# Two expert layers behind an attention: the first layer's weight loads are placed earlier, its first copies get another buffer, and the output words' low parts change engine

## The chip, the cores and the metric

One Trainium2 chip, one core of it. The metric is the device time of one execution in microseconds (us), the median of several runs. A core has five engines that run their own instruction lists in order and wait for each other by semaphores: TensorE (PE; its weight loads are PEld), VectorE (DVE), ScalarE (ACT), GpSimd (POOL) and SyncE (SP), which here issues nearly all DMA transfers. A row "SPq" is SP's sequencer issuing a transfer; the transfer itself goes on after it.

## The reference

```python
def _attn_ref(q, k, v, M_prev, z_prev, beta):        # 4 x 8 heads x 576 x 64
    scores = causal(q @ k.T / sqrt(D)); a = softmax(scores); local = a @ v
    q_p = elu(q) + 1
    mem_out = (q_p @ M_prev) / (q_p @ z_prev + 1e-6)
    return sigmoid(beta) * mem_out + (1 - sigmoid(beta)) * local

def _moe_ref(x, w_gate, w_val, w_out):               # x: 2304 x 512
    return sigmoid(x @ w_gate) * (x @ w_val) @ w_out # 512 x 1536, 512 x 1536, 1536 x 512

def _moe2_ref(x, w_gate, w_val, w_out):
    g = x @ w_gate
    return g * sigmoid(g) * (x @ w_val) @ w_out
```

The weights arrive as 64-bit floats and the kernel turns them into 32-bit ones itself. It computes each matrix product as three passes over a high and a low part of each factor (high by high, high by low, low by high).

## The kernel before

Attention comes first, with the first layer's value product for part of the tokens and the turning of its gate and value weights woven in; turned weights are **kept** in DRAM (`ws`), and value results as words in DRAM (`vs`). Then come four stages on which this text rests:

**Blocks of layer 1** (`blocks`, from L844). 24 runs: for each of six weight pairs p (256 columns of the gate or value weights) three gate runs and one value run over 768 tokens each. A run is seven products (Strassen's scheme; `product`, L828), each of six matmuls of 128 x 128 by 128 x 384. A run has three of eight PSUM banks. What frees a bank is a copy on ACT into a tile c0, c1 or c2 (`keep`, L874), an addition on DVE (`add`, L877), or the finish: the sigmoid on ACT (L837) and a multiplication on DVE (L839 by value words loaded as `vi`, L841 by the other run's result). Finished results are stored (`hs`, L845).

What else has to be done meanwhile stands in a table `at`: a step under the number n is emitted after product n of the list. Products of one weight pair p are numbered b = 28p and on. Per pair there are four such jobs:

- V: load of the kept value weights (`kept`, L595, two transfers `raw<-ws`), two sums steps (L633, L634, L637, L638, on DVE), and eight splits: high parts on ACT (L31, `wset`), low parts on DVE (L654);
- G: the same for the next pair's gate weights;
- W0 and W1: two output words (128 rows of `w_out`) loaded raw (L487), turned by one ACT step (L500) and DVE steps (L503 and L504, L507, L511), and stored (`ws<-a`, L562).

All four jobs load into two buffers `raw` by turns, so a load on SP waits until the job before the last has read its buffer for the last time; everything behind it in SP's list waits too. Inside this stage the emission order is binding on every engine (`pinned`).

**Output of layer 1** (`outputs`, L974): for each of six token tiles twelve words m; the words are loaded two at a time (L582; the last two raw, L487) and put as a high part (ACT, L31) and a low part (L603, on POOL) into places of a matmul operand that has come free (`xop`, `wset`). **Blocks and output of layer 2** are built alike (PE lines L828 and L971) with loads from DRAM in another pattern.

Tiles lie in pools that are opened and closed like a stack. A pool that is opened over the place of a closed one waits, tile by tile, for the last use of that place. At the start of the blocks of layer 1 the pool `m_h` (five tiles h of 3 KB per partition) is opened first, and `m_c` (c0, two c1, c2, 1.5 KB each) behind it.

Of the kernel before, what the change touches and what calls it, by code (L numbers as in the profile page):

```python
ENGINE = {'wh': 'act', 'xh': 'pool', 'vo': 'act', 'ml': 'pool', 'p0': 'act', 'p3': 'act', 'e': 'dve', 'p2': 'any', 'x': 'act', 'mh': 'pool', 'p4': 'dve', 'w': 'pool', ('head', 'w'): 'pool', 'xl': 'pool', ('rest', 'e'): 'act', ('rest', 'p4'): 'act', 'p1': 'act', 'th': 'act', 'uh': 'act', ('rest', 'x'): 'any', ('head', 'n3'): 'pool', 'n3': 'pool', ('rest', 'n4'): 'pool', ('rest', 'n3'): 'pool', ('head', 'n1'): 'pool', 'n4': 'dve', ('head', 'p3'): 'dve', ('rest', 'p3'): 'act', ('head', 'n0'): 'dve', 'oh': 'act', 'ol0': 'dve', 'ol1': 'dve', 'xg': 'act', 'xm': 'dve', 'w00': 'dve', 'w01': 'dve', 'w10': 'dve', 'w11': 'dve', 'hv': 'dve'}
WHEN = {'qk': -2.918, 'zm': -2.8, 'v': -0.622, 'pe': -1.766, 'pw': -1.489, 'pm': -1.092, 't0': -0.87, 't1': -0.45, 'te': 0.857, 's3': 0.004, 's2': 0.265, 's4': 0.5, 's1': 0.704, 's0': 0.85, 'p3': 0.476, 'p2': 0.809, 'p4': 0.938, 'p1': 0.919, 'p0': 1.1, 'v0': 1.112, 'v1': 1.339, 'store': 1.26, ('rest', 'v0'): 1.425, ('rest', 's4'): 0.378, ('head', 'v'): -1.263, ('rest', 'p1'): 0.628, ('rest', 's1'): -0.002, ('head', 'v0'): 1.122, ('rest', 'store'): 2.346, ('head', 's2'): 0.45, ('rest', 's0'): 0.08, ('head', 's4'): 0.733, ('rest', 'v1'): 1.114, ('rest', 'zm'): -2.421, ('rest', 'te'): 0.827, ('rest', 'pw'): -1.506}
WHEN0 = {'pm': -1.252, 'pe': -1.0, 'pw': -0.99, 'zm': -2.0, 't0': -1.2, 's0': 0.834, 'te': 0.682}
SPAN = {'head': (0.8, 0.85), 'rest': (0.734, 0.75), 'full': (0.866, 1.0)}
# [2 lines left out]
REUSE = dict(reuse_waits="tile")  # L7
# [11 lines left out]
F32 = mybir.dt.float32  # L19
# [20 lines left out]
def either(nc, name):  # L40
    return nc.gpsimd if ENGINE.get(name, "pool") == "pool" else nc.vector

# [431 lines left out]
class Weights:  # L474
# [123 lines left out]
    def put(self, l, m, s, t, a):  # L598
        def high():
            copy(self.nc, "wh", t[:, 0], a)  # L600

        def low():
            either(self.nc, "wl").tensor_sub(t[:, 1], a, t[:, 0].bitcast(F32))  # L603
            self.ready[l, m, s] = t.rearrange("p a (k f) -> p a k f", f=128)

        return [high, low]
# [67 lines left out]
class Moe:  # L674
# [344 lines left out]
    def run(self, att, banks):  # L1019
        nc, MC, NP, NJ, T = self.nc, self.MC, self.NP, self.NJ, self.T  # L1020
# [55 lines left out]
            return do  # L1076

        with ExitStack() as tiles:
            self.hp = self.pool("m_h", 5, tiles, **REUSE)
            self.cs = _Bufs(self.pool("m_c", 1, tiles, **REUSE), dict(c0=1, c1=2, c2=1))  # L1080
            top = ExitStack()
            self.scr = self.pool("m_scr1", 4, top, **REUSE)

            runs = []
            for p in range(NP):
                order = [(0, 0), (0, 2), (1, 2), (0, 1)] if p == 0 else [(0, 0), (0, 1), (0, 2), (1, 2)]
                runs += [Run(0, s, p, j, sets, s == 0 and j < 2) for s, j in order]
            at = {}

            steps = self.right(self.from_dram(1), 1, xo[2])  # L1090
            for half, a, b in ((steps[:8], 6, 12), (steps[8:], 15, 21)):
                put(at, half[:1], a - 6 if a < 15 else a - 2, a)
                put(at, half[1:], a, b)
            for p in range(NP):

                b = 28 * p
                if p:
                    turning, splits = prepare(0, p, 1)
                    put(at, turning[:1], b + 3, b)
                    put(at, turning[1:], b + 7, b + 9)  # L1100
                    put(at, splits, b + 10, b + 18)
                    load, turn = W.keep_output(0, 2 * p - 2, False)
                    put(at, load, b + 4, b)
                    put(at, turn, b + 9, b + 15)
                if p + 1 < NP:
                    turning, splits = prepare(0, p + 1, 0)
                    put(at, turning[:1], b + 18, b)
                    put(at, turning[1:], b + 22, b + 24)
                    put(at, splits, b + 25, b + 30)
                if p:  # L1110
                    load, turn = W.keep_output(0, 2 * p - 1, False)
                    put(at, load, b + 19, b)
                    put(at, turn, b + (23 if p + 1 < NP else 21), b + (30 if p + 1 < NP else 25))

            put(at, [spots_in(lambda: xo[2].tile([128, 7, 2, 2, T], F32R, tag="x", name="xop"), spot, 0, 9)],
                b + 18, b)
            put(at, [spots_in(slot(1), spot, 9, 3)], b + 25, b)
            put(at, [lambda: self.over(top, 2)], b + 21, b)
            pairs = [W.outputs(0, m, spot.get) for m in range(0, 10, 2)]
            words = [W.output(0, m, spot.get) for m in (10, 11)]  # L1120
            put(at, [pairs[0][0]], b + 19, b)
            put(at, pairs[0][1:], b + 24, b + 26)
            put(at, [pairs[1][0]], b + 27, b)
            self.prelude(at, b + 21, (0, 1, 6, 6), (5, 6))
            with self.pinned():
                self.blocks(runs, at)
                at = {}
                for m in range(2, 10):
                    put(at, [pairs[m // 2][1 + m % 2]], m - 2, 0)
                for i in range(2, 5):  # L1130
                    put(at, [pairs[i][0]], 2 * i - 5 if i > 2 else 0, 0)
                put(at, [words[0][0]], 5, 0)
                put(at, words[0][1], 7, 9)
                put(at, [words[1][0]], 7, 0)
                put(at, words[1][1], 9, 10)
                for j, b in ((0, 27), (1, 49)):
                    put(at, self.right(lambda k, j=j: [[self.yb[j, k + 2 * c][:, i] for i in range(2)] for c in range(2)],
                                       j, xo[j]), b, b + 8)
                put(at, [lambda: W.plan(pieces)], 11, 0)
                turning, splits = prepare(1, 0, 0)  # L1140
                put(at, turning, 13, 19)
                put(at, splits, 20, 26)
                turning, later = prepare(1, 0, 1)
                put(at, turning, 66, 71)
                self.hin = [(self.hb, "h")] * 2 + [(self.cs, "c0"), (self.cs, "c1"), (self.cs, "c1"), (self.cs, "c2")]
                self.outputs(0, at)
            top.close()


        with ExitStack() as tiles:  # L1150
            self.hp = self.pool("m_h2", 6, tiles, **REUSE)
            self.cs = _Bufs(self.pool("m_c2", 1, tiles, **REUSE), dict(c0=1, c1=2, c2=1))
            top = ExitStack()
            self.scr = self.pool("m_scr3", 2, top, **REUSE)
            at = {}
# [134 lines left out]
```

## Time and profile before

| what | us |
|---|---|
| median of three runs (lowest, highest) | 1194.44 (1189.36, 1196.86) |
| the profiled execution, its own time | 1190.62 |
| its span, first to last instruction | 1188.8 |
| blocks of layer 1 (first to last product) | 383.81 to 608.94 |
| output of layer 1, first tile | 608.77 to 639.40 |
| blocks of layer 2, their first products and last run left out | 771.43 to 1023.31 |

PE is busy for 94% of the span, DVE for 67%, ACT for 50%, POOL for 17%. The granted TensorE clock is 0.973 of full speed on the mean. Because a run's last two products stand among the next run's first, PE's first run has five; so the windows of 28 products in the rows below begin two products behind the product b of their pair. The timelines give the start of a group from the start of the span, its length, the engine, the line, the operation, and in brackets how long the engine had been idle before it and what ended that.

### The profile page before, as it was taken

How to read it: one execution, taken by the hardware profiler on the slowest of the kernel's cores; microseconds unless marked ns; L12 is line 12 of the kernel's file. 1: busy time of each engine (PE TensorE's matmuls, PEld its weight loads, DVE VectorE, ACT ScalarE, POOL GpSimd, SP SyncE). 2: the span in 40 equal slices, each digit the busy share in tenths (PEclk: the TensorE clock that was granted, in tenths of full speed). 3: DMA queues.
4: the chain of work that ended last, by engine and by line, in shares of the span. 5: the costliest groups of instructions: out<-in, count | busy, mean ns of one | idle time of the engine just before them, and what ended most of it. 6: DMA issues, size and time to landing. Idle time of an engine off the chain costs nothing.

```text
span 1188.8 us, 19143 instructions
## 1 busy us (share of the span) xinstructions
PE 1113.9 (94%) x6416; PEld 1002.2 (84%) x6416; DVE 798.2 (67%) x1996; ACT 597.1 (50%) x1470; POOL 197.3 (17%) x233
## 2 busy tenths in 40 slices
PE   7889999998999779889989999999999999899998
PEld 5577787776879778788879999899999999878887
DVE  7898868788669566766756646487878878443332
ACT  5666766675667544544433434355455455332222
POOL 3585533443330000000031000000000000220000
PEclk9799999997999889999999999999999999999999
DMA  5566546546324446465475432423443542654443
GB/s 138 161 204 180 152 126 177 152 127 191 91 61 133 164 155 193 165 221 154 180 230 174 133 99 81 147 90 114 157 133 120 164 129 102 196 176 124 125 123 104
DMA packets 162355, 173.77 MB, mean 146 GB/s; under 512 B 69328, under 2 KB 127696, under 8 KB 162256
## 3 DMA queue, kind: packets, MB, share of 16 engines
q1 hardware_dynamic: 162112, 172.54, 47.3%
q8 instruction: 51, 0.84, 0.3%
q14 instruction: 48, 0.39, 0.1%
q10 hardware_dynamic: 144, 0.00, 0.0%
HBM read 112.20 MB, written 60.29 MB: 145 GB/s over the span
## 4 chain that ended last, share of the span: by engine, by line
PE 60%; DVE 11%; DMA 11%; ACT 4%; issue 3%; SPq 1%; POOL 1%; POOLq 0%; ACTq 0%; DVEq 0%
PE ps L828 22%; PE ps L971 12%; PE ps L974 11%; PE gv L742 5%; DMA raw<-in_moe_w_out_dram 4%; PE sc L316 3%; PE av L396 2%; DVE c L877 2%; PE tp L363 1%; DVE wset L654 1%; DMA hd<-hs 1%; DMA raw<-ws 1%; DMA raw<-in_moe_w_gate_dram 1%; ACT h L837 1%; DVE h L839 1%
## 5 line engine op out<-in xcount | busy, mean ns | idle before, releaser
L828 PE MATMUL ps<-xop,wset 128*128 128x384 f32 x2520 | 454.6, 340 | 39.3 <-ACT c L874 29.0
L828 PEld LDWEIGHTS ps<-xop,wset 128*128 128x128 f32 x2520 | 444.8, 190 | 48.3 <-ACT c L874 37.0
L957 DVE TENSOR_TENSOR hl<-hd,hl 128x384 fp32r<-128x384 f32 x144 | 83.1, 577 | 160.9 <-ACT hl L956 160.3
L956 ACT CAST hl<-hd 128x384 fp32r<-128x384 f32 x144 | 74.0, 514 | 188.8 <-PE ps L971 90.2
L874 ACT COPY c<-ps 128x384 f32<-128x384 f32 x180 | 85.9, 478 | 117.2 <-PE ps L828 112.2
L742 PE MATMUL gv<-x,w 128*128 128x256 f32 (+2 forms) x720 | 127.9, 321 | 3.6 <-POOL x L33 2.0
L877 DVE TENSOR_TENSOR c<-ps,c 128x384 f32<-128x384 f32 x180 | 99.7, 554 | 46.0 <-ACT c L874 24.2
L742 PEld LDWEIGHTS gv<-x,w 128*128 128x128 f32 x720 | 109.2, 196 | 13.4 <-issue 4.7
L974 PE MATMUL ps<-hl,xop 128*128 128x384 f32 x648 | 114.6, 337 | 0.5 <-POOL xop L603 0.5
L974 PEld LDWEIGHTS ps<-hl,xop 128*128 128x128 f32 x648 | 112.7, 188 | 1.1 <-POOL xop L603 1.1
L971 PE MATMUL ps<-xop,hl 128*128 128x512 f32 x486 | 111.5, 389 | 0.7 <-POOL xop L603 0.7
L971 PEld LDWEIGHTS ps<-xop,hl 128*128 128x128 f32 x486 | 91.3, 188 | 20.1 <-POOL xop L603 1.1
L837 ACT ACTIVATE h<-c 128x384 f32<-128x384 f32 x108 | 56.7, 525 | 82.0 <-DVE c L877 81.8
L338 POOL TENSOR_SCALAR s<-s,sum,omg 128x512 f32<-128x512 f32 (+2 forms) x92 | 72.5, 797 | 109.2 <-DVE sum L334 29.7
L330 ACT ACTIVATE s<-s,nm 128x256 f32<-128x256 f32 (+3 forms) x128 | 71.8, 563 | 18.6 <-DVE nm L319 17.5
L316 PE MATMUL sc<-qka 64*128 64x384 f32 (+3 forms) x384 | 71.9, 373 | 5.1 <-DVE nm L319 3.0
L500 ACT ACTIVATE a<-raw 128x512 f32<-128x512 f32 x72 | 48.4, 672 | 56.4 <-DMA raw<-in_moe_w_out_dram 27.4
L319 DVE CUSTOM_DVE_ANT_0 s<-sc,mask 128x256 f32<-128x256 f32 (+3 forms) x128 | 59.6, 485 | 16.0 <-PE tp L355 8.3
L603 POOL TENSOR_TENSOR xop<-raw,xop 128x512 fp32r<-128x512 f32 x16 | 22.1, 1392 | 280.6 <-PE ps L828 249.8
L603 POOL TENSOR_TENSOR wset<-raw,wset 128x512 fp32r<-128x512 f32 x4 | 5.8, 1455 | 378.5 <-ACT wset L31 378.5
L316 PEld LDWEIGHTS sc<-qka 64*128 64x128 f32 x384 | 46.4, 201 | 21.0 <-issue 5.4
L31 ACT COPY p<-tp 128x512 f32<-128x512 f32 x96 | 44.8, 493 | 24.3 <-PE av L396 12.2
(143 smaller groups left out, 1579.5 us busy)
## 6 DMA issues: line engine op xcount, KB each, us to landing
hs<-h SPq DMA_DIRECT2D x72, 384.0 KB, 2.5
hd<-hs SPq DMA_DIRECT2D x144, 192.0 KB, 2.7
raw<-in_moe_w_val_dram SPq DMA_DIRECT2D x24, 512.0 KB, 4.0
raw<-in_moe_w_gate_dram SPq DMA_DIRECT2D x24, 512.0 KB, 4.4
raw<-in_moe_w_out_dram SPq DMA_DIRECT2D x24, 512.0 KB, 4.6
ws<-a SPq DMA_DIRECT2D x44, 256.0 KB, 2.4
vi<-vs SPq DMA_DIRECT2D x24, 384.0 KB, 7.3
xraw<-xs SPq DMA_DIRECT2D x16, 384.0 KB, 3.8
```

What stands on the lines that cost most here:

```text
L316: nc.tensor.matmul(o, lhsT=qk[hr, x, 0, qs], rhs=qk[hr, y, 1, 0:n], start=k == 0, stop=k == 2)
L330: nc.scalar.activation(out=s, in_=s, func=ACTF.Exp, bias=nm[:, h:h + 1], scale=-1.0, accum_out=sm[:, h:h + 1])
L338: self.two(f"n{i}", u).tensor_scalar(s, s, r[:, h:h + 1], w, op0=ALU.mult, op1=ALU.mult)
L742: nc.tensor.matmul(o, lhsT=w[:, i, k, :], rhs=x[:, j, k, :], start=n == 0, stop=n == 3 * self.KD - 1)
L828: self.nc.tensor.matmul(o, lhsT=w[:, a, i, k], rhs=x[:, b, j, k], start=first and n == 0, stop=n == 5, skip_group_check=True)
L837: nc.scalar.activation(out=h, in_=src, func=ACTF.Silu if r.l else ACTF.Sigmoid)
L874: nc.scalar.copy(r.c[n], r.banks[0])
L877: nc.vector.tensor_add(r.c[n], r.banks[bank], r.c[n])
L956: nc.scalar.copy(hl[:, 0], h)
L957: nc.vector.tensor_sub(hl[:, 1], h, hl[:, 0].bitcast(F32))
L971: nc.tensor.matmul(y, lhsT=h[:, i, 128 * c:128 * c + 128], rhs=w[:, j].rearrange("p k f -> p (k f)"), **st)
L974: nc.tensor.matmul(y[:, 0:T], lhsT=w[:, i, c, :], rhs=h[:, j, :], **st)
```

## The change

Four edits:

1. `wl2`: the low parts of the output words (L603, 12 in each layer) go from POOL to DVE.
2. The pool `m_c` is opened ahead of `m_h` (in both layers), so the c tiles and the h tiles exchange places in memory.
3. In the blocks of layer 1 the four jobs get other numbers (below).
4. The first two pairs of output words are loaded two and three products earlier (157 and 164 for 159 and 167).

| job | load | sums, or ACT step to last DVE step | splits |
|---|---|---|---|
| W0 before | b+4 | b+9 to b+15 | |
| W0 now | b-1 | b+6 to b+12 | |
| V before | b+3 | b+7, b+9 | b+10 to b+18 |
| V now | b+3 | b+9, b+10 | b+11 to b+16 |
| W1 before | b+19 | b+23 to b+30 | |
| W1 now | b+13 | b+19 to b+26 (last pair b+23) | |
| G before | b+18 | b+22, b+24 | b+25 to b+30 |
| G now | b+16 | b+22, b+24 | b+25 to b+30 |

```diff
-ENGINE = {..., 'hv': 'dve'}
+ENGINE = {..., 'hv': 'dve', 'wl2': 'dve'}
...
         def low():
-            either(self.nc, "wl").tensor_sub(t[:, 1], a, t[:, 0].bitcast(F32))
+            either(self.nc, f"wl{s}").tensor_sub(t[:, 1], a, t[:, 0].bitcast(F32))
...
+            self.cs = _Bufs(self.pool("m_c", 1, tiles, **REUSE), dict(c0=1, c1=2, c2=1))
             self.hp = self.pool("m_h", 5, tiles, **REUSE)
-            self.cs = _Bufs(self.pool("m_c", 1, tiles, **REUSE), dict(c0=1, c1=2, c2=1))
...
                 if p:
+                    load, turn = W.keep_output(0, 2 * p - 2, False)
+                    put(at, load, b - 1, b)
+                    put(at, turn, b + 6, b + 12)
                     turning, splits = prepare(0, p, 1)
                     put(at, turning[:1], b + 3, b)
-                    put(at, turning[1:], b + 7, b + 9)
-                    put(at, splits, b + 10, b + 18)
-                    load, turn = W.keep_output(0, 2 * p - 2, False)
-                    put(at, load, b + 4, b)
-                    put(at, turn, b + 9, b + 15)
+                    put(at, turning[1:], b + 9, b + 10)
+                    put(at, splits, b + 11, b + 16)
+                    load, turn = W.keep_output(0, 2 * p - 1, False)
+                    put(at, load, b + 13, b)
+                    put(at, turn, b + 19, b + (26 if p + 1 < NP else 23))
                 if p + 1 < NP:
                     turning, splits = prepare(0, p + 1, 0)
-                    put(at, turning[:1], b + 18, b)
+                    put(at, turning[:1], b + 16, b)
                     put(at, turning[1:], b + 22, b + 24)
                     put(at, splits, b + 25, b + 30)
-                if p:
-                    load, turn = W.keep_output(0, 2 * p - 1, False)
-                    put(at, load, b + 19, b)
-                    put(at, turn, b + (23 if p + 1 < NP else 21), b + (30 if p + 1 < NP else 25))
...
-            put(at, [pairs[0][0]], b + 19, b)
+            put(at, [pairs[0][0]], b + 17, b)
             put(at, pairs[0][1:], b + 24, b + 26)
-            put(at, [pairs[1][0]], b + 27, b)
+            put(at, [pairs[1][0]], b + 24, b)
```

The same exchange of `self.cs` and `self.hp` is made in layer 2 (`m_c2`, `m_h2`). Three places of the instruction lists show what it moves.

**ACT, the end of the fill and the first run of the blocks, before** (vo: value words of the fill; c0_5441: the first run's first copy; what an instruction waits for stands in brackets, DMAHW being a DMA's landing):

```order
L31 COPY vo_5325<-gv_5312 128x384 [waits DMAHW6_49,PE_49,Activation_49]
L31 CAST wset_5383<-wsum_5378 128x256 [waits DVE_49]
L31 CAST wset_5383<-raw_5375 128x256 [waits DVE_49]
L31 CAST wset_5383<-wsum_5378 128x256 [waits DVE_49]
L874 COPY c0_5441<-ps_5415 128x384 [waits DMAHW2_49,PE_49,Activation_49]
L837 ACT_TABLE_LOAD
L837 ACTIVATE h_5418<-c0_5441 128x384 [waits DVE_49]
```

Now:

```order
L31 COPY vo_5325<-gv_5312 128x384 [waits DMAHW6_49,PE_49,Activation_49]
L31 CAST wset_5383<-wsum_5378 128x256 [waits DVE_49]
L874 COPY c0_5441<-ps_5415 128x384 [waits PE_49]
L31 CAST wset_5383<-raw_5375 128x256 [waits DVE_49]
L31 CAST wset_5383<-wsum_5378 128x256 [waits DVE_49]
L837 ACT_TABLE_LOAD [waits DVE_49]
L837 ACTIVATE h_5418<-c0_5441 128x384 [waits Activation_49]
```

The copy no longer waits for a landing, and it stands two casts further ahead.

**SP, one weight pair in the middle of the blocks (p = 3), before** (a: a turned word on its way to `ws`):

```order
L562 DMA ws_59<-a_6322 128x512
L845 DMA hs_60<-h_6212 128x768
L595 DMA raw_6420<-ws_59 128x4x128 x2
L487 DMA raw_6431<-in_moe_w_out_dram 128x1024
L845 DMA hs_60<-h_6211 128x768
L845 DMA hs_60<-h_6373 128x768
L845 DMA hs_60<-h_6372 128x768
L562 DMA ws_59<-a_6484 128x512
L845 DMA hs_60<-h_6452 128x768
L595 DMA raw_6590<-ws_59 128x4x128 x2
L487 DMA raw_6600<-in_moe_w_out_dram 128x1024
```

Now:

```order
L562 DMA ws_59<-a_6278 128x512
L487 DMA raw_6371<-in_moe_w_out_dram 128x1024
L855 DMA vi_6394<-vs_58 128x768
L855 DMA vi_6396<-vs_58 128x768
L845 DMA hs_60<-h_6218 128x768
L595 DMA raw_6422<-ws_59 128x4x128 x2
L845 DMA hs_60<-h_6217 128x768
L845 DMA hs_60<-h_6377 128x768
L562 DMA ws_59<-a_6448 128x512
L845 DMA hs_60<-h_6376 128x768
L487 DMA raw_6536<-in_moe_w_out_dram 128x1024
L595 DMA raw_6574<-ws_59 128x4x128 x2
```

Before, V and W0, and G and W1, are issued back to back. Now each word is issued ahead of its weights, with other transfers between; the store of the word before stands right ahead of W0's load.

**DVE, the same pair, V's two sums steps, before** (L877 lines are the additions into c tiles):

```order
L841 TENSOR_TENSOR h<-h,c_6340 128x384
L633 TENSOR_TENSOR wsum<-raw 128x256
L634 TENSOR_TENSOR wsum<-wsum,raw 128x256
L877 TENSOR_TENSOR c_6459<-ps,c_6459 128x384
L839 TENSOR_TENSOR h<-h,vi 128x384
L877 TENSOR_TENSOR c_6471<-ps,c_6471 128x384
L637 TENSOR_TENSOR raw<-raw 128x2x128
L638 TENSOR_TENSOR wsum<-raw,wsum 128x256
L839 TENSOR_TENSOR h<-h,vi 128x384 x2
L654 TENSOR_TENSOR wset<-raw,wset 128x256
```

Now:

```order
L841 TENSOR_TENSOR h<-h,c_6343 128x384
L877 TENSOR_TENSOR c_6461<-ps,c_6461 128x384
L503 TENSOR_SCALAR a<-a 128x512
L504 TENSOR_SCALAR a<-a 128x512
L839 TENSOR_TENSOR h<-h,vi 128x384
L877 TENSOR_TENSOR c_6470<-ps,c_6470 128x384
L633 TENSOR_TENSOR wsum<-raw 128x256
L634 TENSOR_TENSOR wsum<-wsum,raw 128x256
L839 TENSOR_TENSOR h<-h,vi 128x384 x2
L507 SCALAR_TENSOR_TENSOR a<-raw,a 128x512
L637 TENSOR_TENSOR raw<-raw 128x2x128
L638 TENSOR_TENSOR wsum<-raw,wsum 128x256
```

The instruction that waits for V's landing (L633) stood ahead of the two additions of this stretch and stands behind them now; W0's DVE steps have moved in between.

## Rows read from the trace of the kernel before

**Rows 1.** Six weight pairs' products alone (window, length, PE, PEld, clock, DMA share, GB/s):
```profile
383.81:425.25 41.44, 32.39 (x168) 31.16 (x169) 0.92 0.46 156
425.25:465.04 39.79, 32.22 (x169) 31.25 (x169) 0.91 0.58 189
465.04:501.20 36.16, 30.71 (x169) 29.10 (x169) 1.00 0.53 182
501.20:536.25 35.05, 30.71 (x168) 29.11 (x169) 1.00 0.57 188
536.25:572.74 36.49, 32.12 (x168) 30.84 (x169) 0.95 0.55 181
572.74:608.94 36.20, 30.60 (x169) 28.99 (x168) 1.00 0.55 180
```

**Rows 2.** The chain of waits, layer 2's blocks (start, length, what):
```profile
771.43 251.89 PE ps L828 x1440
```

**Rows 3.** Timeline of PE, 383 to 640 us (start, length, operation, idle before and releaser):
```profile
393.15 19.01 PE L828 MATMUL ps<-xop,wset 128*128 128x384 f32 x96 [7.09 <-ACT c L874]
...
417.56 17.34 PE L828 MATMUL ps<-xop,wset 128*128 128x384 f32 x96 [0.66 <-ACT c L874]
440.74 19.17 PE L828 MATMUL ps<-xop,wset 128*128 128x384 f32 x96 [5.84 <-DVE c L877]
461.48 3.40 PE L828 MATMUL ps<-xop,wset 128*128 128x384 f32 x18 [1.56 <-ACT c L874]
...
606.57 2.37 PE L828 MATMUL ps<-xop,wset 128*128 128x384 f32 x12 [2.23 <-ACT c L874]
```

**Rows 4.** Waits between engines, 380 to 640 us (total, times, longest):
```profile
DVE wsum L633 <- DMA raw<-ws: 32.8, 9, 8.4
ACT a L500 <- DMA raw<-in_moe_w_out_dram: 27.4, 9, 5.0
```

**Rows 5.** Timeline of ACT, 383 to 440 us: around the first copy:
```profile
387.19 0.41 ACT L31 CAST wset<-wsum 128x256 fp32r<-128x256 f32 x1
...
392.62 0.48 ACT L874 COPY c<-ps 128x384 f32<-128x384 f32 x1 [4.01 <-DMA vs<-vo]
393.11 1.28 ACT L837 ACT_TABLE_LOAD   x1
```

**Rows 6.** Timeline of SP: G's loads of one pair, V's of the next:
```profile
452.26 1.24 SPq L595 DMA_DIRECT2D raw<-ws  x2
...
469.75 1.23 SPq L595 DMA_DIRECT2D raw<-ws  x2
```

**Rows 7.** Timeline of DVE, 440 to 505 us:
```profile
467.68 0.69 DVE L511 SCALAR_TENSOR_TENSOR a<-raw,a 128x512 int32<-128x512 int32 x1
...
475.88 0.42 DVE L633 TENSOR_TENSOR wsum<-raw 128x256 f32<-128x256 f32 x1 [5.51 <-DMA raw<-ws]
```

**Rows 8.** Timeline of ACT, 440 to 505 us: W1's first step, second pair:
```profile
460.02 0.66 ACT L500 ACTIVATE a<-raw 128x512 f32<-128x512 f32 x1 [4.31 <-DMA raw<-in_moe_w_out_dram]
```

**Rows 9.** DMA issues, 383 to 645 us (count, KB each, median us to landing):
```profile
raw<-in_moe_w_out_dram SPq DMA_DIRECT2D x12, 512.0 KB, 6.0
raw<-ws SPq DMA_DIRECT2D x20, 256.0 KB, 3.5
```

**Rows 10.** DMA issues, 418 to 420 us:
```profile
vi<-vs SPq DMA_DIRECT2D x2, 384.0 KB, 3.4
```

**Rows 11.** DMA issues, 454.6 to 458 us:
```profile
vi<-vs SPq DMA_DIRECT2D x4, 384.0 KB, 7.9
```

**Rows 12.** Windows (length, PE, PEld, DVE, ACT, POOL busy, clock, DMA, GB/s):
```profile
440.00:450.00 10.00, 9.26 (x40) 9.26 (x41) 9.12 (x22) 6.50 (x16) 0.00 (x0) 0.72 0.21 83
608.77:639.40 30.63, 28.19 (x146) 26.58 (x146) 14.86 (x22) 12.51 (x24) 13.76 (x10) 0.94 0.72 239
```

**Rows 13.** The page, costliest groups (busy us, mean ns, idle before and releaser):
```profile
L603 POOL TENSOR_TENSOR xop<-raw,xop 128x512 fp32r<-128x512 f32 x16 | 22.1, 1392 | 280.6 <-PE ps L828 249.8
```

**Rows 14.** Timeline of all engines, 596 to 645 us:
```profile
602.93 1.78 DVE L511 SCALAR_TENSOR_TENSOR a<-raw,a 128x512 int32<-128x512 int32 x1
```

More of the change, by code (lines that the diff above doesn't have):

```diff
@@ L1 @@
-ENGINE = {'wh': 'act', 'xh': 'pool', 'vo': 'act', 'ml': 'pool', 'p0': 'act', 'p3': 'act', 'e': 'dve', 'p2': 'any', 'x': 'act', 'mh': 'pool', 'p4': 'dve', 'w': 'pool', ('head', 'w'): 'pool', 'xl': 'pool', ('rest', 'e'): 'act', ('rest', 'p4'): 'act', 'p1': 'act', 'th': 'act', 'uh': 'act', ('rest', 'x'): 'any', ('head', 'n3'): 'pool', 'n3': 'pool', ('rest', 'n4'): 'pool', ('rest', 'n3'): 'pool', ('head', 'n1'): 'pool', 'n4': 'dve', ('head', 'p3'): 'dve', ('rest', 'p3'): 'act', ('head', 'n0'): 'dve', 'oh': 'act', 'ol0': 'dve', 'ol1': 'dve', 'xg': 'act', 'xm': 'dve', 'w00': 'dve', 'w01': 'dve', 'w10': 'dve', 'w11': 'dve', 'hv': 'dve'}
+ENGINE = {'wh': 'act', 'xh': 'pool', 'vo': 'act', 'ml': 'pool', 'p0': 'act', 'p3': 'act', 'e': 'dve', 'p2': 'any', 'x': 'act', 'mh': 'pool', 'p4': 'dve', 'w': 'pool', ('head', 'w'): 'pool', 'xl': 'pool', ('rest', 'e'): 'act', ('rest', 'p4'): 'act', 'p1': 'act', 'th': 'act', 'uh': 'act', ('rest', 'x'): 'any', ('head', 'n3'): 'pool', 'n3': 'pool', ('rest', 'n4'): 'pool', ('rest', 'n3'): 'pool', ('head', 'n1'): 'pool', 'n4': 'dve', ('head', 'p3'): 'dve', ('rest', 'p3'): 'act', ('head', 'n0'): 'dve', 'oh': 'act', 'ol0': 'dve', 'ol1': 'dve', 'xg': 'act', 'xm': 'dve', 'w00': 'dve', 'w01': 'dve', 'w10': 'dve', 'w11': 'dve', 'hv': 'dve', 'wl2': 'dve'}
 WHEN = {'qk': -2.918, 'zm': -2.8, 'v': -0.622, 'pe': -1.766, 'pw': -1.489, 'pm': -1.092, 't0': -0.87, 't1': -0.45, 'te': 0.857, 's3': 0.004, 's2': 0.265, 's4': 0.5, 's1': 0.704, 's0': 0.85, 'p3': 0.476, 'p2': 0.809, 'p4': 0.938, 'p1': 0.919, 'p0': 1.1, 'v0': 1.112, 'v1': 1.339, 'store': 1.26, ('rest', 'v0'): 1.425, ('rest', 's4'): 0.378, ('head', 'v'): -1.263, ('rest', 'p1'): 0.628, ('rest', 's1'): -0.002, ('head', 'v0'): 1.122, ('rest', 'store'): 2.346, ('head', 's2'): 0.45, ('rest', 's0'): 0.08, ('head', 's4'): 0.733, ('rest', 'v1'): 1.114, ('rest', 'zm'): -2.421, ('rest', 'te'): 0.827, ('rest', 'pw'): -1.506}
@@ L1150, in run @@
         with ExitStack() as tiles:
+            self.cs = _Bufs(self.pool("m_c2", 1, tiles, **REUSE), dict(c0=1, c1=2, c2=1))
             self.hp = self.pool("m_h2", 6, tiles, **REUSE)
-            self.cs = _Bufs(self.pool("m_c2", 1, tiles, **REUSE), dict(c0=1, c1=2, c2=1))
             top = ExitStack()
```

## The prediction

> **What bounds the kernel now.** First I looked where TensorE (PE) doesn't run through. Layer 2's blocks show its full pace: the chain of waits has 1440 matmuls in one piece of 251.89 us [rows 2], 0.1749 us each, so 1.05 us for a product of six and 29.4 us for the 168 matmuls of a weight pair. The same products in layer 1's blocks, cut by weight pair, take 35 to 41 us [rows 1]: 225.13 us where 6 x 29.4 = 176.3 would do, 48.8 us over (by pair 12.0, 10.4, 6.8, 5.7, 7.1 and 6.8). This stage is what the change is about.
>
> Second, the timeline of PE [rows 3] shows what ends its stops: a copy on ACT or an addition on DVE that frees a PSUM bank. Neither engine is behind by its own work; the table of waits says what they stood for: DVE's first sums step L633 for kept weights (32.8 us in 9 waits), ACT's first turning step L500 for an output word (27.4 us in 9) [rows 4]. Both engines run in order, so a late transfer holds the copies and additions behind it. One case of each: L633 idles 5.51 us before 475.88 [rows 7], L500 4.31 us before 460.02 [rows 8], and PE stops 1.56 us at 461.48 [rows 3]. The longest stop, 7.09 us at 393.15, is another matter [rows 3]: there the first copy waits for the landing of a value store from memory that its tile c0 takes over [rows 5].
>
> Third, the DMA issues say how long such a transfer takes: 6.0 us median for a word, 3.5 us for a half of the kept weights [rows 9], where the old numbers leave four to five products (4.2 to 5.3 us) from load to use.
>
> **The change, part by part.**
>
> *First copy.* It loses the wait for the landing and two casts ahead of it. It could start when the cast at 387.19 is done, at 387.60, instead of 392.62 [rows 5]: 5.0 us. After the long stop the granted clock is down: 96 matmuls from 393.15 take 19.01 us, 96 from 417.56 take 17.34 us [rows 3]; with a stop of some 2 us in its place I take the 1.7 us as gained too. Against it: ACT's table load of 1.28 us [rows 5], with two casts (0.41 each), a sigmoid of about 0.5 and the second copy (0.48), now ends near 391.2, where the product that needs this copy could start at 388.1 + 2 x 1.05 = 390.2: 1.0 us of a new wait that lay under slow products before. Sum **-5.7 us**; ends -3.5 (the clock falls all the same, and the tokens' words for the next operand come later than the faster products want them) and -8.8 (7.09 + 1.7).
>
> *The loads of pairs 2 to 6.* These pairs take 183.7 us, 36.7 over 5 x 29.4 [rows 1]. W0 is now loaded seven products ahead of its first step and W1 six, 7.35 and 6.3 us against a landing of 6.0, and no longer right behind V or G, which made the 6.0. V has six products (it had four), G six (four). V's load stands where it stood, behind a store that waits for DVE; but DVE was some 4 us behind there: the third pair's V was issued at 469.75 [rows 6], seven products after product b, which starts two products (some 2.4 us) ahead of that pair's window [rows 1], because of the stop at 460 [rows 8]. Without that stop it comes near product 4.5, and is wanted by DVE behind product b+9, near 10.5 x 1.05, some 6 us later. On DVE the two additions that PE waits for now stand ahead of L633, so V may be about 2 us late before PE notices. What stays: the last pair's PE busy time of 30.60 is without stops, and still 1.2 over the pace [rows 1]; I leave that in four pairs, and 2.5 us in pair 2, where two `vi` loads that wait for buffers of the run before stand ahead of V. So 36.7 - 4 x 1.2 - 2.5: **-29.4 us**. Ends: -36.7 (nothing stays) and -15 (half of it comes back, see the rivals).
>
> Here a row has to be weighed against a rule. A `vi` transfer took 3.4 us in a quiet stretch [rows 10] and 7.9 us behind G's two halves, a word and a store (1.4 MB), all issued from 452.26 on [rows 6, 11]: 4.5 us for what stands ahead. Ahead of V now go W0 and two `vi`, 1.25 MB, but over about five microseconds, in which most of it should be through; I take 1.5 to 2 us of delay, which fits into the slack. The Trainium skill ("DMA: Bandwidth & Descriptors", section "Queues, rings and completion order") says that all transfers of SP's queue lie on the same rings and each engine takes a ring's descriptors in order. By that rule spreading the loads frees nothing by itself: V would still have all of W0 and `vi` to let pass, the whole 4.5 us, and the sum of this part would be near -18.
>
> *Low parts on DVE.* GpSimd loses L603: 1.39 us each [rows 13]. DVE gains 12 in each layer; its nearest row of that width, with two inputs, is 0.69 us [rows 7], so 8.3 us a layer. In layer 1 the cover is DVE's idle time in the first output tile, 30.63 - 14.86 = 15.8 us [rows 12]. If that cover were gone, 8.3 us would be the price; I take nothing. The gain: that tile's 144 matmuls need 25.2 us at full pace and take 30.63 [rows 12], 5.4 over; a word's buffer comes free 0.7 us earlier, and the next load on SP waits for just that. Half, **-2.7 us**; ends 0 and -5.4. Beside GpSimd's first low parts an L511 took 1.78 us instead of 0.69 [rows 7, 14], and the stop of 2.23 us at 606.57 follows it [rows 3]; it is counted in the last pair. In layer 2's blocks PE never waits for DVE [rows 2]; taken as nothing, ends +2 and -2.
>
> *Words loaded two and three products earlier*: inside the last pair, counted there. The exchange of pools in layer 2 is taken as nothing: what waits there is the first h tile, and that stays where a store's landing is awaited.
>
> Sum: -5.7 - 29.4 - 2.7 = **-37.8 us**, from the profiled execution's 1190.62 to 1152.8. That execution lies 3.8 us under the median of the three shown; from the median it would be 1156.6. I say **1154**.
>
> **The rivals.**
>
> 1. *V lands late* (chance 0.13). V has to let W0 and two `vi` pass and lands the whole 4.5 us later than alone [rows 10, 11], at 3.5 + 4.5 = 8 us after its issue, about 2 us beyond the 6 at which DVE wants it, and with DVE's own delay PE loses 2.2. For it speaks the spread of rows 10 and 11, against it that the bytes ahead of V are issued over a longer time. Five pairs x 2.2: -37.8 + 11, **1165**. It is what the Trainium skill's rule above would do here.
>
> 2. *DVE becomes the bound* (0.10). Between two second-bank additions of V's stretch (b+8 to b+15) now stand 20 DVE instructions: additions, multiplications, sums, low parts and the four steps of W0. A full stretch of DVE shows 22 in 10 us with 9.12 busy [rows 12], so 20 take about 9.1, where seven products last 7.35. The 1.8 us are meant to go into the slack of three products before PE wants the second addition; if waits for ACT in between use that up, each of five pairs loses some 2.3 us: also near **1165**.
>
> 3. *The loads come no earlier* (0.08). SP is in order: W0's load stands behind the store of W1, which waits for DVE's last step, and V behind an `hs` store. If DVE stays as late as at 469.75 [rows 6], landing and use move together and only the first copy and the low parts count: -8.4, about **1184**.
>
> 4. *Slower* (0.03). With two buffers used by turns, G's load waits for V's last split, and behind it on SP wait the next pair's `vi` words. These are wanted eleven products (11.6 us) later and land in up to 7.9 us [rows 11]: 3.7 us of V's lateness are covered. From there each microsecond comes back as a stop of the next pair, which makes its V late again. The price is what V is late beyond 3.7: at the longest V wait of now, 8.4 [rows 4], 4.7 us in each of five pairs; to lose 12 us net it takes 50, so 14 us of lateness, and the time would be **1207** or more. Nothing in the rows comes near that.
>
> The forecast keeps 0.66, with a range of its own of 1143 to 1163. What a measurement of this kernel can tell from no change is about 1%, 12 us. Faster by more than that: the forecast, rivals 1 and 2, and a third of rival 3, **0.92**; within 1%: the rest of rival 3, **0.05**; slower **0.03**. The range of **1143 to 1174** goes from the gains' far ends together to past rivals 1 and 2 with a few microseconds more of lost slack; rivals 3 and 4 and a tenth of the others lie outside.
>
> **What would show it.** First copy: ACT's copy starts near 387.6 with no landing as its releaser, and the first pair takes about 35.7 us. Loads: L633 and L500 lose nearly all of their 32.8 and 27.4 us of waits in this stage, pairs 3 to 6 take 30 to 31 us each, pair 2 about 32, the clock's mean there is 1.00. Low parts: no GpSimd instruction after attention, the first output tile at about 28 us. It would be wrong if PE still stopped at b+10 to b+13 of each pair for an addition on DVE (rivals 1 and 2: L633 waiting for a landing tells the first from the second), or if V's issue still came seven products after its pair's start (rival 3).

## The result, and the profile after

The changed kernel takes **1156.67 us** (median of four runs, 1152.21 to 1159.61) against 1191.90 (1188.42 to 1196.86) for the kernel before: ratio 0.970, 95% interval 0.965 to 0.975. The forecast was 1154, its range 1143 to 1174. The profiled execution took 1159.61, its span is 1157.8.

The six weight pairs' products, as in [rows 1] (window, length, PE, PEld, clock, DMA share, GB/s):

```profile
392.40:429.40 37.00, 30.90 (x168) 29.06 (x169) 1.00 0.51 174
429.41:463.45 34.04, 31.11 (x170) 30.79 (x170) 0.95 0.64 207
463.45:492.75 29.30, 29.30 (x169) 29.30 (x169) 1.00 0.67 226
492.75:522.06 29.31, 29.31 (x169) 29.31 (x169) 1.00 0.66 224
522.06:551.37 29.31, 29.31 (x170) 29.31 (x170) 1.00 0.66 225
551.37:581.74 30.37, 29.74 (x169) 29.10 (x168) 1.00 0.69 232
```

Pairs 3 to 5 now run at the pace of layer 2 (29.4 us a pair), PE busy for the whole window. What is left over that pace is in pair 1 (7.6 us), pair 2 (4.7) and pair 6 (1.0). The timeline of PE, the counterpart of [rows 3], shows where:

```profile
396.62 2.38 PE L828 MATMUL ps<-xop,wset 128*128 128x384 f32 x12 [1.97 <-ACT c L874]
400.22 7.58 PE L828 MATMUL ps<-xop,wset 128*128 128x384 f32 x42 [1.21 <-ACT c L874]
408.38 7.58 PE L828 MATMUL ps<-xop,wset 128*128 128x384 f32 x42 [0.58 <-ACT c L874]
417.64 3.44 PE L828 MATMUL ps<-xop,wset 128*128 128x384 f32 x18 [1.69 <-ACT c L874]
421.74 22.58 PE L828 MATMUL ps<-xop,wset 128*128 128x384 f32 x126 [0.65 <-ACT c L874]
447.24 131.51 PE L828 MATMUL ps<-xop,wset 128*128 128x384 f32 x744 [2.92 <-ACT c L874]
579.38 2.36 PE L828 MATMUL ps<-xop,wset 128*128 128x384 f32 x12 [0.62 <-ACT c L874]
```

The stop of 7.09 us has become one of 1.97, and from 447.24 on PE runs 131.51 us without a stop that the timeline shows. The table of waits (total, times, longest), for [rows 4]:

```profile
DVE wsum L633 <- DMA raw<-ws: 3.8, 1, 3.8
ACT a L500 <- DMA raw<-in_moe_w_out_dram: 2.3, 3, 1.2
ACT xop L31 <- DMA xraw<-xs: 6.7, 6, 3.1
```

60.2 us of waiting for the two kinds of loads have become 6.1; the one long wait left for kept weights is pair 2's V. What stops the first pair behind its first copies is the third line, words of the next operand's tokens. DMA issues from 393 to 582 us (count, KB each, median us to landing), for [rows 9]:

```profile
raw<-ws SPq DMA_DIRECT2D x20, 256.0 KB, 4.3
raw<-in_moe_w_out_dram SPq DMA_DIRECT2D x10, 512.0 KB, 3.9
```

A word lands in 3.9 us where it took 6.0; a half of kept weights takes 4.3 where it took 3.5, and only pair 2's V is still waited for. The first output tile, for the second row of [rows 12]:

```profile
581.58:608.80 27.22, 26.09 (x145) 24.80 (x145) 18.01 (x32) 11.64 (x23) 0.00 (x0) 1.00 0.76 253
```

By stages, the blocks from their first product to the end of their last and the others what lies between, in the profiled executions of before and after: attention and fill 383.81 and 392.40, blocks of layer 1 225.1 and 189.3, its output 134.7 and 131.4, blocks of layer 2 289.0 and 288.7, the rest 156.2 and 156.0. The part ahead of the blocks got 8.6 us longer though its instructions are the same; more on that below.

### The profile page after: what moved, and what is told of

Read it like the earlier page. It is cut to its first block, busy times and chain, and to the rows that moved or that the text cites. A ratio compares the mean times of both kernels' runs of the same rounds, so it can differ in the third digit from the quotient of the medians.

```text
span 1157.8 us, 19120 instructions
## 1 busy us (share of the span) xinstructions
PE 1111.7 (96%) x6416; PEld 1004.8 (87%) x6416; DVE 805.5 (70%) x2020; ACT 599.9 (52%) x1470; POOL 164.2 (14%) x209
## 4 chain that ended last, share of the span: by engine, by line
PE 76%; DMA 6%; DVE 5%; ACT 2%; issue 1%; SPq 0%; ACTq 0%; DVEq 0%
PE ps L828 34%; PE ps L971 13%; PE ps L974 11%; PE gv L742 6%; PE sc L316 3%; PE av L396 3%; DMA xraw<-xs 2%; PE tp L363 2%; PE sc L302 1%; DMA hd<-hs 1%; PE av L387 1%; DMA raw<-ws 1%; DMA raw<-in_moe_w_gate_dram 1%; PE tp L254 1%; PE tp L355 1%
## 5 line engine op out<-in xcount | busy, mean ns | idle before, releaser
L828 PE MATMUL ps<-xop,wset 128*128 128x384 f32 x2520 | 445.6, 337 | 12.3 <-ACT c L874 12.3
L957 DVE TENSOR_TENSOR hl<-hd,hl 128x384 fp32r<-128x384 f32 x144 | 80.3, 558 | 151.8 <-ACT hl L956 150.8
L956 ACT CAST hl<-hd 128x384 fp32r<-128x384 f32 x144 | 74.0, 514 | 189.0 <-PE ps L971 84.7
L742 PE MATMUL gv<-x,w 128*128 128x256 f32 (+2 forms) x720 | 131.3, 327 | 3.5 <-ACT vo L31 1.7
L877 DVE TENSOR_TENSOR c<-ps,c 128x384 f32<-128x384 f32 x180 | 99.6, 554 | 43.6 <-ACT c L874 20.2
L742 PEld LDWEIGHTS gv<-x,w 128*128 128x128 f32 x720 | 112.4, 202 | 13.0 <-issue 6.8
L316 PE MATMUL sc<-qka 64*128 64x384 f32 (+3 forms) x384 | 74.8, 386 | 4.5 <-DVE nm L319 2.2
L500 ACT ACTIVATE a<-raw 128x512 f32<-128x512 f32 x72 | 48.4, 673 | 33.7 <-DMA raw<-in_moe_w_gate_dram 19.5
L507 DVE SCALAR_TENSOR_TENSOR a<-raw,a 128x512 int32<-128x512 int32 x72 | 53.3, 740 | 0.2
L511 DVE SCALAR_TENSOR_TENSOR a<-raw,a 128x512 int32<-128x512 int32 x72 | 50.3, 698 | 0.3
```

What stands on the lines that cost most here:

```text
L316: nc.tensor.matmul(o, lhsT=qk[hr, x, 0, qs], rhs=qk[hr, y, 1, 0:n], start=k == 0, stop=k == 2)
L742: nc.tensor.matmul(o, lhsT=w[:, i, k, :], rhs=x[:, j, k, :], start=n == 0, stop=n == 3 * self.KD - 1)
L828: self.nc.tensor.matmul(o, lhsT=w[:, a, i, k], rhs=x[:, b, j, k], start=first and n == 0, stop=n == 5, skip_group_check=True)
L877: nc.vector.tensor_add(r.c[n], r.banks[bank], r.c[n])
L956: nc.scalar.copy(hl[:, 0], h)
L957: nc.vector.tensor_sub(hl[:, 1], h, hl[:, 0].bitcast(F32))
```

## The experiments

The table sums up the profiled executions of all kernels: start of the blocks, the six pairs, their sum, all in us, then the median of all runs.

| kernel | start | 1 | 2 | 3 | 4 | 5 | 6 | sum | median |
|---|---|---|---|---|---|---|---|---|---|
| before | 383.8 | 41.4 | 39.8 | 36.2 | 35.1 | 36.5 | 36.2 | 225.1 | 1190 to 1195 |
| changed | 392.4 | 37.0 | 34.0 | 29.3 | 29.3 | 29.3 | 30.4 | 189.3 | 1156.7 |
| changed, again | 388.1 | 37.5 | 34.3 | 29.3 | 29.3 | 29.3 | 30.4 | 190.2 | 1153.6 |
| jobs alone | 381.0 | 41.3 | 35.4 | 29.3 | 29.3 | 29.3 | 30.4 | 195.0 | 1158.9 |
| pools alone | 385.8 | 37.1 | 40.1 | 34.7 | 36.4 | 35.2 | 36.4 | 220.0 | 1188.1 |
| low parts alone | 384.2 | 41.0 | 40.9 | 33.2 | 36.5 | 39.6 | 36.1 | 227.3 | 1185.5 |
| V's uses alone | 379.0 | 40.3 | 39.8 | 34.7 | 37.5 | 35.0 | 38.9 | 226.3 | 1192.6 |
| changed, V's uses old | 384.2 | 37.8 | 35.1 | 31.5 | 30.7 | 31.2 | 31.7 | 198.1 | 1157.2 |
| changed, words later | 386.6 | 38.1 | 36.1 | 29.3 | 29.3 | 29.3 | 30.4 | 192.5 | 1155.6 |
| old load order, uses later | 392.6 | 36.8 | 35.7 | 33.5 | 33.7 | 32.2 | 34.9 | 206.9 | 1176.0 |
| changed, five buffers | 387.9 | 36.8 | 30.7 | 29.3 | 29.3 | 29.3 | 30.4 | 185.8 | 1148.0 |
| changed, table load early | 383.0 | 38.2 | 32.5 | 29.3 | 29.3 | 29.3 | 30.4 | 189.0 | 1152.5 |
| five buffers, tokens early | 384.5 | 33.6 | 30.6 | 29.4 | 29.3 | 29.3 | 30.4 | 182.6 | 1144.6 |

The start scatters by 13.6 us over kernels whose instructions are the same up to there, so I judge each edit by its own stage and use the medians only where they differ by more. The medians come from four groups of runs; each group has its own runs of the kernel before, with medians of 1190.3 to 1194.7, and a ratio is taken to those.

**One edit at a time.** Jobs alone, that is the changed kernel with its first two edits undone; the new numbers and the words' earlier loads stay.

```diff
-ENGINE = {..., 'wl2': 'dve'}
+ENGINE = {...}
 # m_h opened ahead of m_c again, in both layers
```

> Only the new numbers of the four jobs and of the first two word pairs; the first copies' memory and the engine of the low parts stay as before. My theory (the transfers now land ahead of their use, and that is worth 29 to 33 us in pairs 2 to 6): 1192 - 31 = 1161, between 1158 and 1165; first pair still 40 to 42 us, pairs 3 to 6 about 29.5 to 30.5 each, pair 2 near 34, first output tile 29 to 31. Rival (the three edits help each other, for instance the low parts on GpSimd hold the words' buffers and so the last pair's loads, and the long first stop makes pair 2's loads late): above 1168, with pair 2 over 36 or pair 6 over 33.

1158.9 (ratio 0.974, 0.969 to 0.979). Pairs 2 to 6 took 153.7 us where before took 183.7: 30.0 less. Pair 1 is untouched; pair 2 took 35.4, 1.4 over the forecast. The theory holds, the edits don't need each other for this part.

Pools alone, in layer 1:

```diff
+            self.cs = _Bufs(self.pool("m_c", 1, tiles, **REUSE), dict(c0=1, c1=2, c2=1))
             self.hp = self.pool("m_h", 5, tiles, **REUSE)
-            self.cs = _Bufs(...)
```

> Only the exchange of the pools m_c and m_h in layer 1's blocks. My theory: the first copy no longer waits for a value store's landing, the first pair goes from 41.4 to about 37 us, the rest stays: 1192 - 4.5 = 1187.5, between 1185 and 1190. Rival (the landing only moves to the first h tile, which the sigmoid waits for, and PE stops one product later): within 1.5 us of before, first pair 40 to 41.5.

The first pair took 37.14, 4.3 less, with one stop of 2.00 us in the place of 7.09; the stage shows it, the time doesn't (ratio 0.998, 0.994 to 1.002), since the start alone scatters more.

Low parts alone:

```diff
-            either(self.nc, "wl").tensor_sub(...)
+            either(self.nc, f"wl{s}").tensor_sub(...)     # 'wl2': 'dve'
```

> Only the output words' low parts on VectorE instead of GpSimd, in both layers. My theory: first output tile from 30.6 to about 27.5 us, and the stop of 2 us before it goes with GpSimd's work beside VectorE: 1192 - 4.5 = 1187.5, between 1185 and 1191. Rival (the first tile got faster through the words' earlier loads, not through the engine): within 1.5 us of before, first output tile still 30 to 31.

Its first output tile, in the columns of the row above, and from the timeline of PE the stop at the end of the last pair:

```profile
611.55:638.90 27.35, 25.88 (x145) 24.60 (x144) 18.00 (x32) 12.33 (x24) 0.00 (x0) 1.00 0.78 251
```
```profile
609.20 2.36 PE L828 MATMUL ps<-xop,wset 128*128 128x384 f32 x12 [0.62 <-ACT c L874]
```

From its first product (611.39) to the next tile's (638.94) the tile took 27.55 us, where the kernel before took 30.51 between the same points: 3.0 less. The stop of 2.23 us is 0.62. With the jobs alone, low parts still on GpSimd, the tile took 30.1, so its gain is the engine's (over all kernels 29.9 to 30.7 us with GpSimd, 27.0 to 27.6 with VectorE); but the stop was 0.62 there too, so either edit removes that one. The time itself can't tell (0.997, 0.993 to 1.001).

**What in the jobs makes the gain: V's place on DVE, or the loads?** First V's uses alone, in the kernel before:

```diff
-                    put(at, turning[1:], b + 7, b + 9)
-                    put(at, splits, b + 10, b + 18)
+                    put(at, turning[1:], b + 9, b + 10)
+                    put(at, splits, b + 11, b + 16)
```

> The kernel before, with the value weights' uses alone at their new numbers (sums b+9 and b+10, splits b+11 to b+16), behind the two additions; all loads and all words stay. My theory (half of the loss comes from words that land late because they are issued behind the weights, and these stay): 4 to 10 us less in the blocks of layer 1, 215 to 221 us instead of 225; L500's waits stay above 20 us. Rival (the order on VectorE alone makes the gain): 20 us or more less, 205 or below.

Neither came: 226.3 us for the blocks, nothing gained (ratio 1.002, 0.998 to 1.006). The table of waits says where it went:

```profile
ACT a L500 <- DMA raw<-in_moe_w_out_dram: 46.8, 11, 7.0
DVE wsum L633 <- DMA raw<-ws: 16.0, 7, 4.8
PE ps L828 <- ACT c L874: 37.3, 24, 6.4
```

L633's waits fell from 32.8 to 16.0 us, L500's rose from 27.4 to 46.8 [rows 4]. In the kernel before 14 of PE's waits here ended on a copy on ACT (26.1 us) and 4 on an addition on DVE (9.7); now all 24 end on ACT (37.3). I read it so: PE, no longer stopped for V, comes sooner to the stop for the word that is loaded behind V.

Then the other way round, the changed kernel with V's uses at their old numbers:

```diff
-                    put(at, turning[1:], b + 9, b + 10)
-                    put(at, splits, b + 11, b + 16)
+                    put(at, turning[1:], b + 7, b + 9)
+                    put(at, splits, b + 10, b + 16)
```

> The changed kernel, with the value weights' sums steps at their old numbers b+7 and b+9 and their splits from b+10 on, so that L633 stands again ahead of the two additions that PE waits for. My theory (what counts is that the transfers have landed: V lands near 4.5 us after its issue at b+1 to b+3, two products before the old place): 1 to 4 us above the changed kernel, so 1158 to 1161, nearly all of it in pair 2 whose V lands late. Rival (the gain comes from the place of L633 behind the additions, and the transfers are as late as before): 10 to 15 us above, 1167 to 1172, with 2 to 3 us more in each of pairs 2 to 6.

8.7 us more in the blocks, 1.0 to 2.2 in each of pairs 2 to 6, between the two theories; the median (1157.2 against 1156.7) doesn't show it. The rows of SP and DVE in pair 3 show why mine fell short:

```profile
460.17 1.24 SPq L595 DMA_DIRECT2D raw<-ws  x2
460.96 0.56 DVE L841 TENSOR_TENSOR h<-h,c 128x384 f32<-128x384 f32 x1
465.70 0.42 DVE L633 TENSOR_TENSOR wsum<-raw 128x256 f32<-128x256 f32 x1 [4.18 <-DMA raw<-ws]
```

I had V issued at b+1 to b+3 and L633 reached behind product b+7. The pair's window begins at 457.06, two products after product b. So V was issued five products after product b began, later than I had it. And what stands ahead of L633 is done at 461.52, 6.3 products after product b began, earlier than I had it and 1.35 us after V's issue; DVE then waits 4.18 us, with the addition that PE needs behind it. A step's number says when it is emitted, not when its engine gets there.

**Must words go ahead, and how far?** Words later, with four products from load to first step as before:

```diff
-                    put(at, load, b - 1, b)         # W0
+                    put(at, load, b + 2, b)
-                    put(at, load, b + 13, b)        # W1
+                    put(at, load, b + 15, b)
```

> The changed kernel, with the output words loaded later: W0 at b+2 instead of b-1, right ahead of V's load, W1 at b+15 instead of b+13, right ahead of G's; both then have four products from load to first step, as before the change. My theory (only landing against use counts; a word alone lands in 3.6 to 4.3 us, four products are 4.2): L500 waits 0 to 1 us each time, pairs 3 to 6 take 29.3 to 30.5 each, the blocks of layer 1 189 to 194 us instead of 189.3. Rival (it is the distance between words and weights that makes the landings short): words and V land in 5.5 to 6.5 us again, L500 waits 10 us or more in all, pairs 3 to 6 take 31 to 32.5 each, the blocks 197 to 203 us.

Pairs 3 to 5 took 29.3 each: four products are enough there. The landings were nearer to the rival's (4.9 to 5.9 us for W0 in pairs 2 to 6), and L500 did wait 16.2 us in 7 cases, which my figure missed. 6.2 of it came at one time, in pair 2, which took 36.1 us instead of 34.0; in pairs 3 to 6 PE never stopped for it.

The old order of the loads, with the uses moved back instead:

```diff
+                    put(at, load, b + 4, b)         # W0, right behind V's load at b + 3
+                    put(at, turn, b + 11, b + 16)
...
+                    put(at, load, b + (17 if p + 1 < NP else 19), b)    # W1, behind G's at b + 16
+                    put(at, turn, b + (24 if p + 1 < NP else 21), b + (31 if p + 1 < NP else 25))
```

> The changed kernel, with the loads in the old order and places (V b+3, then W0 b+4; G b+16, then W1 b+17) and with the uses later instead: V at b+9 on, W0's first step b+11, W1's b+24; the last pair's W1 and word pairs at their old numbers. My theory (the number of products between load and use is what counts, six or seven here, not the order of words and weights): pairs 3 to 5 take 29.3 to 30.5 each, as in the changed kernel, pair 2 33 to 36. Rival (words must go ahead of their weights, apart from them): a word behind V lands in 6 us or more and V's own landing stays near 5, pairs 3 to 5 take 32 to 34 each.

The rival was right on the pairs and on the words, and I was wrong: pairs 3 to 5 took 33.5, 33.7 and 32.2 us. DMA issues of its blocks, the waits, and the timeline of one word's first step in pair 3 on ACT and of PE behind it:

```profile
raw<-ws SPq DMA_DIRECT2D x20, 256.0 KB, 3.5
raw<-in_moe_w_out_dram SPq DMA_DIRECT2D x10, 512.0 KB, 6.0
```
```profile
ACT a L500 <- DMA raw<-in_moe_w_out_dram: 21.1, 9, 4.0
DVE wsum L633 <- DMA raw<-ws: 15.8, 8, 4.8
```
```profile
494.31 0.66 ACT L500 ACTIVATE a<-raw 128x512 f32<-128x512 f32 x1 [3.34 <-DMA raw<-in_moe_w_out_dram]
495.39 7.92 PE L828 MATMUL ps<-xop,wset 128*128 128x384 f32 x44 [1.83 <-ACT c L874]
```

The word behind its weights needs 6.0 us to land, as in the kernel before, and its seven products shrink: SP issues this one at 488.01, four products after its number, behind G's two halves and a store. The edit does more than change the order, though: it also moves W1's last step to b+31, and SP issues V behind the store of that word. In pairs 3 to 5 V went out 5.7 to 6.8 products after product b began, in the changed kernel 5.0, and L633 waited 15.8 us in all instead of 3.8. How the loss divides between the two was not separated.

**What stays in pairs 1 and 2.** Five buffers for the value words:

```diff
-            self.scr = self.pool("m_scr1", 4, top, **REUSE)
+            self.scr = self.pool("m_scr1", 5, top, **REUSE)
```

> The changed kernel, with five instead of four buffers for the value words vi (m_scr1). My theory (what stays in pair 2 is V's load, held on SP behind two vi loads that wait for a buffer): V of pair 2 is issued 1.5 to 3 us earlier against its pair's start, DVE's 3.8 us wait for it falls to under 2, pair 2 takes 30 to 32 us instead of 34.0. Rival (pair 2 is slow from the landing of its W0 or from a DVE that is behind from the first pair): pair 2 still 33.5 to 34.5.

From the timelines, SP's issues and DVE's first V step in pair 2, of the changed kernel and of this one:

```profile
433.52 1.94 SPq L855 DMA_DIRECT2D vi<-vs  x2
436.02 1.62 SPq L595 DMA_DIRECT2D raw<-ws  x2
441.76 0.43 DVE L633 TENSOR_TENSOR wsum<-raw 128x256 f32<-128x256 f32 x1 [3.84 <-DMA raw<-ws]
```
```profile
426.62 2.57 SPq L855 DMA_DIRECT2D vi<-vs  x2
429.75 1.30 SPq L595 DMA_DIRECT2D raw<-ws  x2
435.15 0.42 DVE L633 TENSOR_TENSOR wsum<-raw 128x256 f32<-128x256 f32 x1 [1.88 <-DMA raw<-ws]
```

V goes out 6.6 us after the start of its pair's window with four buffers, 5.0 with five; the pair takes 30.7 instead of 34.0, as forecast.

Table load early:

```diff
+                if i == 0 and r.l == 0:
+                    nc.scalar.activation(out=r.banks[2][:, 0:1], in_=self.X[0].bitcast(F32)[:, 0, 0, 0, 0:1],
+                                         func=ACTF.Sigmoid)
```

> The changed kernel, with one sigmoid of a single column on ACT ahead of the first run, so that ACT's table load of 1.28 us does not stand between the first sums and the second copy. My theory (the stop of 1.2 us at the start of the blocks is the table load): this stop goes, the first pair takes 35.7 to 36.2 us instead of 37.0, and nothing is lost ahead of it, since ACT waits for landings there. Rival (the table load moves into the last copies of the fill and holds them): the first copy's stop of 1.97 us grows by about 1.2 and the first pair stays at 36.8 to 37.3.

Neither range came. The load now stands among the fill's last copies, the first copy comes later, and its stop is 2.89 us instead of 1.97, 0.9 of the 1.2 more that the rival had; but the stop of 1.2 us is gone, as I had it. The first pair took 38.2, more than either said, because its matmuls were slower: the granted clock was 0.91 where it was 1.00 in the changed kernel. PE's idle time in the pair fell all the same, from 6.1 us to 4.9. Pair 2 took 32.5 instead of 34.0, for a reason that stays open, and the blocks 189.0 against 189.3. The row of the first pair (columns of [rows 1]), ACT and PE:

```profile
382.96:421.15 38.19, 33.29 (x168) 32.33 (x169) 0.91 0.52 176
380.57 1.28 ACT L894 ACT_TABLE_LOAD   x1
388.10 12.11 PE L828 MATMUL ps<-xop,wset 128*128 128x384 f32 x57 [2.89 <-ACT c L874]
```

**A faster version**, and the changed kernel again beside it:

```diff
+            self.scr = self.pool("m_scr1", 5, top, **REUSE)
-                put(at, half[:1], a - 6 if a < 15 else a - 2, a)
+                put(at, half[:1], a - 6 if a < 15 else a - 7, a)
```

> The changed kernel with five buffers for the value words (as in the run with five buffers) and with the second half of the tokens' words for the next operand loaded five products earlier (after product 8 instead of 13), ahead of the second hs store. My theory (what stays in the first pair after its first copies is the wait for those words, 3.1 us on ACT and 3.7 on DVE, which stops PE 1.7 and 0.7 us): first pair 36.8 to 34.5 us, pair 2 30 to 31, the blocks 183 to 184 us instead of 189.3, the whole some 5 to 6 us under the changed kernel. Rival (the earlier load waits for a buffer that the first run's value words hold, and the queue behind it with it): first pair 36.5 or more, the blocks 186 or more.

> The changed kernel once more, for the stages' own scatter: the blocks of layer 1 take 188 to 191 us again, layer 2 288.7, and the attention part ahead of them, whose instructions the change doesn't touch, starts the blocks somewhere between 380 and 393 us. If the change did make attention longer (392.4 against 383.8 in the two executions profiled first), they start near 392 again.

1144.6 us (1141.2 to 1146.5; 0.960 of before, 0.955 to 0.965) against 1153.6 (1146.2 to 1158.6; 0.967, 0.961 to 0.972) for the changed kernel. The blocks took 182.55, pair 1 33.56: the two stops for the tokens' words are gone, those of the first copies (1.68, 1.23) stay. The theory held, with somewhat more than it forecast. Against the run with five buffers alone the first pair is 3.3 us shorter, but 2.2 of that is PE's busy time, at a granted clock of 1.00 for 0.95, and only 1.1 its idle time. The changed kernel's second execution started its blocks at 388.1, between the two seen before.

## Why the prediction was right

*First copy*, -5.7 forecast, -4.4 measured (-4.3 with the pools alone). The copy itself started 3.70 us after the stage's first product (3.8 forecast), with no landing behind it, and the stops of about 2 and 1.0 us that I had named are 1.97 and 1.21 (the table load):

```profile
396.10 0.47 ACT L874 COPY c<-ps 128x384 f32<-128x384 f32 x1
...
397.98 1.28 ACT L837 ACT_TABLE_LOAD   x1 [0.78 <-DVE c L877]
```

The mis-sized part is what follows: the tokens' words come later than the faster products want them, the bound I had kept for the range. Three stops stand there, 0.58, 1.69 and 0.65; the load made earlier took away the last two. The kernel before had two, 1.30 and 0.66, so this takes back about 1.0 us. Part of the agreement is luck. I had counted 1.7 us for the clock: here PE was busy for 30.9 us instead of 32.4, at a granted clock of 1.00 for 0.92. With the pools alone, behind a like stop of 2.00, the clock was 0.95, PE was busy for 32.2, and the stop at the table load isn't there; I read it as lying under the slower products:

```profile
385.81:422.95 37.14, 32.18 (x168) 30.40 (x169) 0.95 0.51 174
```

The pair took 37.0 and 37.1 all the same.

*Loads of pairs 2 to 6*, -29.4 forecast, -31.3 measured (-30.0 with the jobs alone). The mechanism was as put. Words no longer behind the weights land in 3.9 us, not 6.0; put back behind them, they need 6.0 again, and 2.9 to 4.6 us are lost in each of pairs 3 to 6; how much of that is V's later issue isn't known. V of pair 3 is issued at 466.55, five products after product b began (4.5 forecast), and landed at 471.73, DVE reaching it at 471.84. The additions ahead of L633 are worth 1.0 to 2.2 us a pair, but only together with the loads: alone they gave nothing. Two sizes were off and cancel in part: I left 1.2 us in each of pairs 3 to 6, and 0.0, 0.0, 0.0 and 1.0 stayed; I left 2.5 in pair 2 for its held `vi` loads, and it was 4.7. The distance of seven and six products was more than needed; in pairs 3 to 5 four do, if the word goes ahead. G's load, two products earlier, and the earlier loads of the last word pairs were not tried alone.

*Low parts*, -2.7 forecast, -3.3 measured (30.51 to 27.22; -3.0 alone). Layer 2 is unchanged, as assumed.

The sum before rounding is -39.1 in these stages, -37.8 forecast. The medians of the two comparisons show -35.2 and -36.7; in the profiled executions the difference lies in the part ahead of the blocks, for the medians that isn't shown. With a part ahead that scatters by 13.6 us, it is partly luck that the median came within 3 us of the forecast.

*Rivals.* V's halves landed 3.2 to 4.7 us after their issue in pairs 3 to 6, not 8: W0 had landed by then, and the last `vi` landed 0.9 to 2.8 us after V's issue (rival 1). DVE held no PE there (rival 2), V's issue moved (rival 3), and nothing was late enough for two buffers to lock (rival 4).

Of the rule from the Trainium skill ("DMA: Bandwidth & Descriptors", section "Queues, rings and completion order": each DMA engine takes the descriptors of a ring in order) the runs say more than I made of it. A word ahead of two `vi` loads landed in 3.6 to 3.9 us in pairs 3 to 6, right behind the two (768 KB) in 4.9 to 5.9 (words later), and right behind the halves of V or G (512 KB) in 5.2 to 6.4 (old load order): what stands ahead is paid for, what stands behind hardly. The trace agrees with the rule in that; the 8 us of rival 1 didn't come, since W0 was issued 4.7 us ahead of V and had landed: the rule bears only on what is still under way.

## What to carry to other kernels

When one queue feeds several engines, load first what is used first and small, and count the time to landing with all that is queued ahead of it. A step's place in a list of products isn't its time: an in-order engine runs ahead to the first instruction that waits, so put instructions that others wait for ahead of one that waits for a transfer. When two waits alternate, removing one can give its time to the other; judge an edit by its stage, not by the whole time, where an untouched stage scatters by more than the edit is worth.

## What the runs showed beside that

The part ahead of the blocks, the same instructions in all kernels but for the early table load, took 379.0 to 392.6 us. Where it was long the granted clock was lower in places: windows of the kernel before (first) and of the changed one (columns as in [rows 12]):

```profile
200.00:240.00 40.00, 38.64 (x267) 30.33 (x267) 29.61 (x109) 26.49 (x79) 14.89 (x20) 0.96 0.49 138
```
```profile
200.00:240.00 40.00, 37.19 (x220) 29.58 (x221) 25.63 (x97) 23.46 (x70) 14.97 (x20) 0.79 0.38 109
```

47 matmuls fewer in these 40 us, with DMA busy for less too. Over the 13 profiled executions the start goes with the mean granted clock between 200 and 379 us, in the main: 0.98 where the blocks start at 379.0, 0.96 and 0.97 at 381.0 and 383.0, 0.95 and 0.94 at 383.8 to 384.5, 0.93 at 385.8 and 386.6, 0.92 at 387.9 and 388.1, 0.90 at 392.4 and 392.6. The earliest (V's uses alone) and the changed kernel:

```profile
200.00:379.00 179.00, 172.04 (x1176) 139.37 (x1177) 140.19 (x442) 118.43 (x328) 60.79 (x76) 0.98 0.44 127
200.00:379.00 179.00, 170.61 (x1106) 135.73 (x1106) 129.23 (x422) 111.28 (x312) 61.61 (x77) 0.90 0.38 111
```

What sets the lower clock off was not tried and stays open. The time of the kernel before alone scatters as much (1183.5 to 1198.1 in 13 executions of one group), so it doesn't take the change. But the kernels with the new numbers started their blocks at 381.0 to 392.4 us and those with the old ones at 379.0 to 385.8 (392.6 with the old load order), so the change isn't cleared of a part of it either.
